# Decoding weights with a parametric relu, loading queries ahead of weights, and another order for the first stage

## The chip, the cores and the metric

The kernel runs on one NeuronCore of one Trainium2 chip. The metric is the device time of one launch in microseconds, lower is better. A time is the median of several runs; beside it stands one execution taken with the hardware profiler, whose rows are read here.

## The reference

```python
# attention over 32 memory slots per head: batch 4, 8 heads, 576 tokens, head_dim 64
a = exp(phi - max over tokens); a = a / (sum over tokens + 1e-09)
k_m = einsum('bhsm,bhsd->bhmd', a, k); v_m = einsum('bhsm,bhsd->bhmd', a, v)
scores = q @ k_m^T / sqrt(64)
attn = softmax(scores) @ v_m                   # tokens: 2304 x 512
x = (attn @ w_a) * (attn @ w_b) @ w_out        # 512 -> 1536 -> 512, gated
h = x @ w_in                                   # 512 -> 2048
out = (h * sigmoid(1.702 * h)) @ w_out2        # 2048 -> 512
```

The attention inputs are float32. The five weight matrices are float64 in memory; the kernel reads them as pairs of 32-bit words.

## The kernel before

**Tiling.** The attention inputs come in eight groups `n = 0..7` (batch `b = n // 2`, four heads each): for each, `phi` (2 DMAs), `k` and `v` (4 DMAs) and `q` (4 DMAs). The weights come in 68 pieces of 128 x 512 elements, called `raw`: 24 of `w_a` and `w_b` together (block `g = 0..5`, four pieces each), 12 of the first output matrix, 16 of `w_in`, 16 of the last one. Each has its own `raw` buffer until it is decoded; there are four such buffers in the first stage.

**Decoding** (`decode_piece`) makes a float32 from the two words of a float64 in four instructions of 128 x 512: ScalarE takes the absolute value of the high word with a scale (L435), VectorE shifts it left by three bits (L437), VectorE puts the sign bit of the high word back (L439), and VectorE adds three bits of the low word (L443).

**Stages.** In the first stage, `memory(n)` and `queries(n)` make the attention of a group, `fold(g, b)` (L791) multiplies the memory values of batch `b` into weight block `g`, and `gated(g, b, u)` (L841, 24 matmuls for each half `u` of the tokens) multiplies the attention by the folded weights; L864 on VectorE multiplies the two results and a DMA stores them (`g1d`). `sum_tokens` (L884, GpSimd) makes sums of them for a Strassen-like product. The second stage (`project`, L1002), the third (`step`, L1277) and the last one (L1478, L1509) are long runs of matmuls. Every matmul is three passes over a high and a low part; `hi_lo` makes these parts with a copy on ScalarE (L341) and a subtraction on VectorE or GpSimd (L335 in `combine`).

**Order.** Nothing is scheduled on the chip. While the program is built, a planner (`Order`) holds a clock for each engine and for the DMAs, gives every instruction an assumed length (`Lengths`, `dve()`, `act()`, `pool()`) and emits instructions in the order in which they would run. Each engine then executes its own list strictly in order, and waits on semaphores where a result isn't there. The SP queue, which issues most DMAs, is such a list too. While nothing else is ready, `warm_up` fills TensorE with small matmuls (L1574) whose result nobody reads, until the first stored result is planned; it holds one of the two PSUM banks of `bank_m`, from which folds and gates also take theirs. `lend_banks` moves banks from the attention's set `bank_a` to `bank_m`. `close_attention` waits for all attention, frees its buffers and marks `close`, after which banks are used in pairs (`pair_up`, `both_free`).

The assumed lengths before are the class's own: 68 ns plus one element a cycle on VectorE. `measured()` sets 150 ns, and further values; it was called at `close` only.

Of the kernel before, what the change touches and what calls it, by code (L numbers as in the profile page):

```python
# [8 lines left out]
F32 = mybir.dt.float32  # L9
# [24 lines left out]
PO1 = 17  # L34
PS1 = 14.8
PT1 = 15
RATE = 330.0, 3000.0
PB1 = 4
PI = 9
# [4 lines left out]
RX = 12  # L44

FIRST = (
    ("phi", 0), ("phi", 1), ("raw", 0), ("kv", 0), ("raw", 1), ("q", 0), ("kv", 1), ("q", 1), ("raw", 2), ("raw", 3),
)


# [22 lines left out]
def dve(n, fast=False):  # L73
    return Lengths.dve + n / (1.92 if fast else 0.96)
# [26 lines left out]
class Order:  # L101
# [9 lines left out]
    def __init__(self):  # L111
        self.clock = {PE: 0.0, ACT: 0.0, DVE: 0.0, POOL: 0.0}
        self.dma, self.marks, self.streams, self.count = 2000.0, {}, [], 0

        self.handicap = {DVE: W0}
        self.rate, self.land = 385.0, 2000.0

    def mark(self, t, *key):
        self.marks[key] = t
# [72 lines left out]
def tile_mem_attention_moe_moe2(  # L192
# [165 lines left out]
    def load(x, n):  # L358
        if x == "raw":
            s = yield "slot", raw_of(n)  # L360
            if s is raw_p and n >= RX:

                od.mark(s[1], "raw_p")
                s = yield "slot", raw_of(n)
            srcs, runs = pieces[n][2:]
            m = 512 // len(srcs)
            for i, src in enumerate(srcs):
                dst = s[0][:, i * m:(i + 1) * m, :]
                (nc.scalar if n < 1 else nc.sync).dma_start(
                    out=dst.rearrange("p (n f) w -> p n (f w)", n=runs), in_=src  # L370
                )
            size = P * 4096
        else:
            s = yield "slot", {"phi": phi_s, "kv": kv_s, "q": q_s}[x]
            if x == "kv":
                for i, src in enumerate((k, v)):
                    load_heads(s[0][:, i], src, n)
            elif x == "phi":
                load_heads(s[0], phi, n, nc.scalar if n == 1 else nc.sync)
            else:  # L380
                b, g = divmod(n, NHG)
                src = q[b].rearrange("(h g) (p c) d -> g h p (c d)", g=NHG, c=QC)[g]
                for h in range(HG):
                    nc.sync.dma_start(
                        out=s[0][h::HG].rearrange("p c d -> p (c d)"), in_=src[h]
                    )
            size = HG * S * {"phi": M, "kv": 2 * D, "q": D}[x] * 4
        loaded[x, n] = s
        od.load(s[1], size, x, n)
# [36 lines left out]
    def decode_piece(t, i, name, part, n, m):  # L426

        raw = loaded.pop(("raw", i))
        lw, hw = (raw[0][:, :, j].rearrange("p (n f) -> p n f", n=n) for j in range(2))
        mf = m[0].rearrange("p (n f) -> p n f", n=n)  # L430
        mu = mf.bitcast(U32)

        slow = Lengths.slow
        t, _ = yield ACT, t, act(512)
        nc.scalar.activation(out=mf, in_=hw.bitcast(F32), func=AF.Abs, scale=2.0 ** -112)  # L435
        t, _ = yield DVE, t, slow * dve(512, True)
        nc.vector.tensor_scalar(out=mu, in0=mu, scalar1=3, scalar2=None, op0=ALU.logical_shift_left)  # L437
        t, _ = yield DVE, t, slow * dve(512)
        nc.vector.scalar_tensor_tensor(  # L439
            out=mu, in0=hw, scalar=0x80000000, in1=mu, op0=ALU.bitwise_and, op1=ALU.bitwise_or  # L440
        )
        t, _ = yield DVE, t, slow * dve(512)
        nc.vector.scalar_tensor_tensor(  # L443
            out=mu, in0=lw, scalar=29, in1=mu, op0=ALU.logical_shift_right, op1=ALU.bitwise_or
        )
        raw_of(i).release(raw, t)
        if name[0] == "wab":
            wt[name] = m
            od.mark(t, *name)
        elif name[0] == "in":  # L450
            decoded[name, part] = m
            od.mark(t, "decoded", name, part)
            if part == 1:
                od.spawn(PW if name[1] else PW0, combine_weights(name[1]))
        elif name[0] == "o2":
            c = name[1]
            t = max(t, (yield "mark", "room", *name))
            t, _ = yield ACT, t, act(DM)
            nc.scalar.activation(out=wo2[c][:, HI], in_=m[0], func=AF.Copy)
            nc.scalar.dma_start(out=w2d[c * P:(c + 1) * P, :], in_=m[0])  # L460
            od.mark(t + 2500.0, "w2d", c)
            t2 = yield from combine(t, wo2[c][:, LO], m[0], f32(wo2[c][:, HI]), ALU.subtract, DM)
            dm_s.release(m, max(t + 2500.0, t2))
            od.mark(t2, "wo2", c)
        else:
            c = name[1]
            decoded[name, 0] = m
            od.mark(t, "decoded", name, 0)
            if c % 4 == 3:
                od.spawn(PS1, combine_out(c // 4))  # L470
# [215 lines left out]

    def lend_banks():

        yield "mark", "attn", 1, 0
        for _ in range(2):  # L690
            s = yield "slot", bank_a
            bank_m.release(s, s[1])

    pair_s = Slots()

    def both_free(i):
        two = [(y, s) for y in (bank_a, bank_m) for s in y.free for x in banks[2 * i:2 * i + 2] if s[0] is x]
        if len(two) < 2:
            return None
        for y, s in two:  # L700
            y.free.remove(s)
        return [s for _, s in two]
# [68 lines left out]
    def fold(g, b):  # L771
# [4 lines left out]
            t = max(t, od.marks["wab", g, r])  # L776
        eff_t[g, b] = s = yield "slot", eff_s
        t = max(t, s[1])
        ps, two = {}, None
        if have("close"):  # L780
            t, two = yield PE, t, 0.0, pair_s
            x = [[two[0][:, c], 0.0] for c in range(NHG)]
        for c in range(NHG):
            if two:
                t, _ = yield PE, t - HOP_PE, (0.0, FOLD / 2)[c]
                ps[c] = x[c]
            else:
                t, ps[c] = yield PE, t - c * HOP_PE, (0.0, FOLD / 2)[c], bank_m
            half = slice(c * D, (c + 1) * D)
            for h in range(HG):  # L790
                nc.tensor.matmul(  # L791
                    ps[c][0][row(h), :], bdv[b][half, h, :], wt["wab", g, h][0][half, :], start=True, stop=True
                )
        for c in range(NHG):
            od.spawn(0, fold_out(t, g, b, c, ps[c], two))
        od.mark(t, "fold", g, b)
# [20 lines left out]
    def gated(g, b, u):  # L817
# [6 lines left out]
            gr_t[g, b] = yield "slot", gr_s  # L824
        gr = gr_t[g, b]
        left, pt, wide = [], [], have("close")
        for j, i in ((0, 0), (1, 0), (0, 1), (1, 1)) if wide else ((0, 0), (0, 1), (1, 0), (1, 1)):
            if True:
                if not wide:
# [19 lines left out]
                if len(pt) == 2:  # L849
                    od.spawn(0, gated_out(g, b, u, slice(0, G1) if wide else slice(j, j + 1), pt, gr, left))  # L850
                    pt = []
        if u == 1:
            eff_s.release(eff_t[g, b], t)

# [752 lines left out]
    with tc.manual_schedule():  # L1607
# [5 lines left out]
            nc.vector.memset(t, 0.0)  # L1613
        make_identity(nc, ident)
        n0 = 2 * NHG
        od.spawn(0, load_all(FIRST))

        nc.scalar.activation(out=zero, in_=zero, func=AF.Exp)
# [48 lines left out]
```

## Time and profile before

| what | value |
|---|---|
| median of 3 runs | 765.1 us (763.99 to 766.24) |
| profiled execution, its own time | 765.62 us |
| its span, first to last instruction | 763.8 us |
| TensorE (PE) busy | 741.0 us, 97% |
| weight loads of TensorE (PEld) | 684.8 us, 90% |
| VectorE (DVE) busy | 615.9 us, 81% |
| ScalarE (ACT) busy | 396.9 us, 52% |
| GpSimd (POOL) busy | 397.3 us, 52% |
| TensorE clock granted | 0.999 of full speed |

Busy TensorE time holds the small filling matmuls too. "PE idle" below is a stretch's length less its PE busy time. The span is 1.8 us shorter than the execution's own time.

### The profile page before, as it was taken

Reading aid. Unit: us, or ns where it says so; the run is one execution under the profiler, and the core shown is the slowest. Engines: PE = TensorE matmul, PEld = TensorE weight load, DVE = VectorE, ACT = ScalarE, POOL = GpSimd, SP = SyncE. Lnnn points to the kernel's source line nnn. Section 1 sums busy time; section 2 is a strip of 40 time slices with the busy share of each in tenths; the row PEclk is TensorE's granted clock in tenths of the full one; section 3 lists DMA queues with packets and bytes.
Section 4 is the critical chain, followed back from the end, with each engine's and each line's share of the span. In section 5 each row is a group of like instructions: output and inputs, shape, how many; then the busy total and the mean of one; then the engine's idle time right before and its main releaser. Section 6 shows DMA issues by size and latency. Waiting matters only on the chain.

```text
span 763.8 us, 14637 instructions
## 1 busy us (share of the span) xinstructions
PE 741.0 (97%) x5360; PEld 684.8 (90%) x5360; DVE 615.9 (81%) x926; ACT 396.9 (52%) x784; POOL 397.3 (52%) x347
## 2 busy tenths in 40 slices
PE   8899999999999989999999999999999999999997
PEld 7676878888788879999989999999998888999997
DVE  4889989699999854974899977767695799998884
ACT  4456654445664354745667555454554456544441
POOL 0213635454987932951899643332151059886661
PEclk9999999999999999999999999999999999999999
DMA  8989583479568796566533845554678956744411
GB/s 256 301 279 313 184 291 136 147 241 317 186 202 256 235 305 192 171 189 189 165 114 101 268 151 181 169 171 147 219 248 278 324 199 190 252 139 139 128 32 36
DMA packets 110360, 153.54 MB, mean 201 GB/s; under 512 B 8400, under 2 KB 89040, under 8 KB 110288
## 3 DMA queue, kind: packets, MB, share of 16 engines
q1 hardware_dynamic: 104832, 143.20, 58.8%
q10 hardware_dynamic: 5456, 9.41, 3.6%
q8 instruction: 42, 0.69, 0.4%
q14 instruction: 30, 0.25, 0.1%
HBM read 100.01 MB, written 52.56 MB: 200 GB/s over the span
## 4 chain that ended last, share of the span: by engine, by line
PE 70%; DVE 9%; DMA 7%; POOL 7%; issue 4%; ACT 2%; SPq 0%; ACTq 0%; DVEq 0%; POOLq 0%
PE bank L1277 23%; PE bank L1509 13%; PE bank L1478 11%; PE bank L1002 11%; PE bank L841 8%; POOL w L335 2%; DMA g1d<-grp 2%; PE bank L791 1%; DMA phi<-in_phi_dram 1%; DVE eff L810 1%; POOL acc L335 1%; DMA acc<-g1d 1%; POOL gr L884 1%; DVE attn L335 1%; DVE acc L439 1%
## 5 line engine op out<-in xcount | busy, mean ns | idle before, releaser
L841 PEld LDWEIGHTS bank<-attn,eff 128*128 128x128 f32 x1152 | 154.5, 188 | 21.2 <-issue 4.4
L841 PE MATMUL bank<-attn,eff 128*128 128x288 f32 x1152 | 165.3, 299 | 2.8 <-DVE acc L864 1.7
L335 POOL TENSOR_TENSOR acc<-acc 128x512 f32<-128x512 f32 (+2 forms) x65 | 95.7, 1494 | 45.0 <-DVE w L335 26.1
L335 DVE TENSOR_TENSOR w<-acc,w 128x512 fp32r<-128x512 f32 (+2 forms) x103 | 106.5, 1060 | 12.4 <-ACT w L341 12.4
L1319 DVE TENSOR_TENSOR acc<-bank,acc 128x384 f32<-128x384 f32 x168 | 88.8, 551 | 32.3 <-PE bank L1277 19.9
L341 ACT ACTIVATE w<-acc 128x512 fp32r<-128x512 f32 (+2 forms) x129 | 74.8, 589 | 51.9 <-PE bank L1509 35.5
L1002 PE MATMUL bank<-attn,w 128*128 128x384 f32 x504 | 93.3, 336 | 3.1 <-DVE attn L335 1.5
L335 DVE TENSOR_TENSOR attn<-acc,attn 128x768 fp32r<-128x768 f32 (+3 forms) x57 | 71.2, 1260 | 28.5 <-ACT attn L341 27.4
L1002 PEld LDWEIGHTS bank<-attn,w 128*128 128x128 f32 x504 | 87.3, 188 | 6.0 <-DVE attn L335 2.8
L341 ACT ACTIVATE attn<-acc 128x768 fp32r<-128x768 f32 (+2 forms) x80 | 61.0, 769 | 53.0 <-PE bank L1002 29.6
L1329 ACT ACTIVATE acc<-acc 128x384 f32<-128x384 f32 x96 | 48.8, 524 | 49.5 <-DVE acc L1319 48.8
L884 POOL TENSOR_TENSOR gr<-gr 128x288 f32<-128x288 f32 x48 | 49.2, 1032 | 31.1 <-DMA g1d<-gr 20.1
L335 POOL TENSOR_TENSOR attn<-acc,attn 128x768 fp32r<-128x768 f32 (+2 forms) x23 | 39.0, 1702 | 47.0 <-ACT attn L341 46.9
L1277 PE MATMUL bank<-attn,w 128*128 128x384 f32 x288 | 55.1, 334 | 0.0
L1277 PEld LDWEIGHTS bank<-attn,w 128*128 128x128 f32 x288 | 50.4, 188 | 0.0
L1002 PE MATMUL bank<-attn,w1b 128*128 128x384 f32 x252 | 48.2, 337 | 1.3 <-DVE attn L335 1.1
L1002 PEld LDWEIGHTS bank<-attn,w1b 128*128 128x128 f32 x252 | 43.8, 188 | 2.8 <-DVE attn L335 2.2
L1277 PE MATMUL bank<-w1b,w 128*128 128x384 f32 x224 | 46.2, 334 | 0.0
L335 POOL TENSOR_TENSOR w<-dm,w 128x256 fp32r<-128x256 f32 x31 | 26.9, 880 | 36.9 <-ACT w L341 36.9
L335 POOL TENSOR_TENSOR w<-acc,w 128x256 fp32r<-128x256 f32 (+2 forms) x24 | 27.4, 1154 | 34.1 <-ACT w L341 34.1
L1277 PE MATMUL bank<-w 128*128 128x384 f32 x224 | 43.8, 334 | 0.0
L1277 PEld LDWEIGHTS bank<-w1b,w 128*128 128x128 f32 x224 | 39.5, 188 | 0.0
(190 smaller groups left out, 1484.7 us busy)
## 6 DMA issues: line engine op xcount, KB each, us to landing
acc<-g1d SPq DMA_DIRECT2D x63, 384.0 KB, 3.8
g2d<-acc SPq DMA_DIRECT2D x96, 192.0 KB, 2.3
raw<-in_moe_w_out_dram SPq DMA_DIRECT2D x24, 512.0 KB, 4.7
acc<-g2d SPq DMA_DIRECT2D x10, 1024.0 KB, 6.7
raw<-in_moe_w_in_dram SPq DMA_DIRECT2D x16, 512.0 KB, 4.4
acc<-g2d SPq DMA_DIRECT2D x16, 512.0 KB, 5.8
g1d<-gr SPq DMA_DIRECT2D x12, 576.0 KB, 3.3
raw<-in_moe_w_a_dram SPq DMA_DIRECT2D x19, 256.0 KB, 4.2
```

Source lines behind the costliest of these rows:

```text
L335: (nc.gpsimd if e == POOL else nc.vector).tensor_tensor(out=dst, in0=in0, in1=in1, op=op)
L341: nc.scalar.activation(out=hi, in_=src, func=AF.Copy)
L439: nc.vector.scalar_tensor_tensor(out=mu, in0=hw, scalar=0x80000000, in1=mu, op0=ALU.bitwise_and, op1=ALU.bitwise_or)
L791: nc.tensor.matmul(ps[c][0][row(h), :], bdv[b][half, h, :], wt["wab", g, h][0][half, :], start=True, stop=True)
L841: nc.tensor.matmul(dst[:, :U], e[:, c, sw, i * CW + j * P:i * CW + (j + 1) * P], attn(b, mv, c, u * U, U), start=(n == 0), stop=(n == 3 * ...
L884: nc.gpsimd.tensor_tensor(out=dst, in0=in0, in1=in1, op=ALU.subtract)
L1002: nc.tensor.matmul(ps[0][:, :N2], w1_of(a, g, sw)[:, r * P:(r + 1) * P], b[0][:, mv, i], start=(first and q == n == 0), stop=(q == NG1 // ...
L1277: nc.tensor.matmul(ps[0][:, :N2], w[:, sw, r, :], y[mv][r], start=(n == 0), stop=(n == 5))
L1319: nc.vector.tensor_tensor(out=s[0], in0=ps[0][:, :N2], in1=x[0], op=ALU.add)
L1329: nc.scalar.activation(out=c[0], in_=c[0], func=AF.Gelu_apprx_sigmoid)
L1478: nc.tensor.matmul(ps[i, s][0], b[0][:, sw, c - o, :], wo2[c][:, mv], start=(c == n == 0), stop=(c == 4 * K4 - 1 and n == 2),)
L1509: nc.tensor.matmul(ps[name][0][:, :NB], x[0][:, sw, c, :], moving(b, h // 2 + c, mv), start=(h == c == n == 0), stop=(h > 0 and c == K4 - ...
```

## The change

The sign step (L439) is gone: the absolute value becomes a parametric relu with a slope of -2^32 for negative inputs, which leaves in the exponent a bit that the shift by three moves into the sign's place. In the table `FIRST` of the first loads, `kv`, `q` of groups 0 and 1 come ahead of all weight pieces; the four DMAs of the first `q` are issued from ScalarE's queue in place of those of the first weight piece. The planner starts with the lengths of `measured()` (with factors of 1.0) and a lower DMA rate. One bank is lent when the first weight block is decoded, the other as before. While a fold or a gate takes single banks, none is taken for a pair.

```diff
+FRONT = 1.0, 1.0, 1.0
+RATE0 = 300.0, 2500.0
...
 FIRST = (
-    ("phi", 0), ("phi", 1), ("raw", 0), ("kv", 0), ("raw", 1), ("q", 0), ("kv", 1), ("q", 1), ("raw", 2), ("raw", 3),
+    ("phi", 0), ("phi", 1), ("kv", 0), ("q", 0), ("kv", 1), ("q", 1), ("raw", 0), ("raw", 1), ("raw", 2), ("raw", 3),
 )
...
-        self.rate, self.land = 385.0, 2000.0
+        self.rate, self.land = RATE0
...
-                (nc.scalar if n < 1 else nc.sync).dma_start(
+                nc.sync.dma_start(
                     out=dst.rearrange("p (n f) w -> p n (f w)", n=runs), in_=src
                 )
...
-                    nc.sync.dma_start(
+                    (nc.scalar if n < 1 else nc.sync).dma_start(
                         out=s[0][h::HG].rearrange("p c d -> p (c d)"), in_=src[h]
                     )
...
-        nc.scalar.activation(out=mf, in_=hw.bitcast(F32), func=AF.Abs, scale=2.0 ** -112)
+        nc.scalar.activation(out=mf, in_=hw.bitcast(F32), func=AF.Prelu, scale=2.0 ** -112, alpha=-2.0 ** 32)
         t, _ = yield DVE, t, slow * dve(512, True)
         nc.vector.tensor_scalar(out=mu, in0=mu, scalar1=3, scalar2=None, op0=ALU.logical_shift_left)
-        t, _ = yield DVE, t, slow * dve(512)
-        nc.vector.scalar_tensor_tensor(
-            out=mu, in0=hw, scalar=0x80000000, in1=mu, op0=ALU.bitwise_and, op1=ALU.bitwise_or
-        )
...
     def lend_banks():
 
-        yield "mark", "attn", 1, 0
-        for _ in range(2):
+        for key in (("wab", 0, 2 * NHG - 1), ("attn", 1, 0)):
+            yield ("mark", *key)
             s = yield "slot", bank_a
             bank_m.release(s, s[1])
 
-    pair_s = Slots()
+    pair_s, single = Slots(), [False]
 
     def both_free(i):
+        if single[0]:
+            return None
...
+        single[0] = not have("close")
         ps, two = {}, None
...
+        single[0] = not wide
...
+        measured()
+        Lengths.pool, Lengths.both, Lengths.slow = FRONT
         od.spawn(0, load_all(FIRST))
```

**The SP queue, from the queries of group 4 on.** `raw_73` here is the eighth weight piece (number 7, the last of block `g = 1`), `phi_95` the next group's `phi`, `g1d<-gr` the stores of the first gate's results. Before:

```order
L384 DMA q_100<-in_q_dram 32x1152 x4
L369 DMA raw_73<-in_moe_w_a_dram 128x512
L369 DMA raw_73<-in_moe_w_b_dram 128x512
L369 DMA raw_74<-in_moe_w_a_dram 128x512
L369 DMA raw_74<-in_moe_w_b_dram 128x512
L869 DMA g1d<-gr 128x2x288
```

Now, with the same loads of group 4 ahead of it:

```order
L386 DMA q_100<-in_q_dram 32x1152 x4
L873 DMA g1d<-gr 128x2x288
L371 DMA raw_73<-in_moe_w_a_dram 128x512
L371 DMA raw_73<-in_moe_w_b_dram 128x512
L873 DMA g1d<-gr 128x288
L352 DMA phi_95<-in_phi_dram 64x4x160
```

The store of gate (0, 0, half 0) has moved ahead of weight piece 7, and that of half 1 ahead of the loads of group 5; pieces 8 and 9 have moved behind group 5.

**TensorE, from the scores of group 1 to the first gate.** L791 is the first fold, in two parts; L841 the first gate; L589 multiplies `k` and `v` of group 2 (`kv_99`, `phi_94`) by its memory weights, and frees the `phi` buffer that group 4 is loaded into; the `ident` matmuls are fillers (L1574) or transposes. Before, in three pieces of that stretch:

```order
L628 MATMUL bank<-qT_108,bdk_93 32x288 x8
L1574 MATMUL bank<-ident 128x128 x8
L548 MATMUL bank<-ident,et_96 128x128 x5
L1574 MATMUL bank<-ident 128x128 x7
L791 MATMUL bank<-acc,gr 32x512 x4
...
L791 MATMUL bank<-acc,gr 32x512 x4
...
L589 MATMUL bank<-kv_99,phi_94 32x128 x20
L548 MATMUL bank<-ident,et_96 128x128 x5
L508 MATMUL bank<-ident,q_101 128x128 x4
L841 MATMUL bank<-attn_81,eff 128x288 x6
```

Now (L626, L546, L792, L844, L587 and L1578 are the same lines, moved):

```order
L626 MATMUL bank<-qT_108,bdk_93 32x288 x8
L1578 MATMUL bank<-ident 128x128 x16
L546 MATMUL bank<-ident,et_96 128x128 x5
L1578 MATMUL bank<-ident 128x128 x2
L792 MATMUL bank<-acc,gr 32x512 x4
L1578 MATMUL bank<-ident 128x128
L792 MATMUL bank<-acc,gr 32x512 x4
...
L1578 MATMUL bank<-ident 128x128 x3
L844 MATMUL bank<-attn_81,eff 128x288 x6
L587 MATMUL bank<-kv_99,phi_94 32x128 x20
```

The two parts of the first fold have moved together, and the first matmuls of the gate stand ahead of the `kv` product of group 2 and not behind it. The whole program has 79 fillers of L1574 instead of 74, and otherwise the same matmuls; each filler is two instructions in the trace.

## Rows read from the trace of the kernel before

**Rows 1.** The page's busy time by engine.
```profile
PE 741.0 (97%) x5360; PEld 684.8 (90%) x5360; DVE 615.9 (81%) x926; ACT 396.9 (52%) x784; POOL 397.3 (52%) x347
```
**Rows 2.** Busy time by stretch, length first, then clock, DMA share, GB/s.
```profile
0.00:64.20 64.20, 55.48 (x689) 45.00 (x689) 46.53 (x116) 33.78 (x84) 12.15 (x19) 1.00 0.88 285
64.20:122.30 58.10, 55.08 (x581) 46.64 (x589) 53.15 (x108) 32.24 (x81) 26.62 (x27) 1.00 0.72 232
122.30:257.60 135.30, 132.81 (x1112) 115.01 (x1112) 121.41 (x166) 69.54 (x124) 91.63 (x82) 1.00 0.66 215
257.60:278.00 20.40, 18.55 (x100) 16.64 (x98) 13.25 (x14) 6.68 (x9) 14.69 (x13) 1.00 0.99 339
278.00:397.00 119.00, 116.51 (x659) 114.04 (x660) 84.45 (x81) 68.80 (x113) 68.95 (x47) 1.00 0.62 180
397.00:764.00 367.00, 362.61 (x2233) 347.42 (x2231) 297.13 (x447) 185.86 (x374) 183.28 (x164) 1.00 0.54 175
```
**Rows 3.** The fillers of L1574 by stretch: PE, then PEld.
```profile
0.00:64.20 64.20, 21.65 (x148) 19.59 (x148) 1.00 0.88 285
```
**Rows 4.** TensorE in order of time: start, length, what.
```profile
37.09 1.06 PE L791 MATMUL bank<-acc,gr 64*32 64x512 f32 x8
...
40.51 1.30 PE L589 MATMUL bank<-kv,phi 128*32 128x128 f32 x40 [0.32 <-ACT phi L326]
...
42.69 1.04 PE L841 MATMUL bank<-attn,eff 128*128 128x288 f32 x6
...
60.76 1.09 PE L791 MATMUL bank<-acc,gr 64*32 64x512 f32 x16
...
64.19 1.04 PE L841 MATMUL bank<-attn,eff 128*128 128x288 f32 x6
```
**Rows 5.** The SP queue in order of time.
```profile
6.57 0.60 SPq L369 DMA_DIRECT2D raw<-in_moe_w_a_dram  x1
...
9.77 2.42 SPq L384 DMA_DIRECT2D q<-in_q_dram  x4
...
41.90 0.64 SPq L350 DMA_DIRECT2D phi<-in_phi_dram  x1
...
49.14 0.52 SPq L369 DMA_DIRECT2D raw<-in_moe_w_a_dram  x1
...
53.14 0.65 SPq L350 DMA_DIRECT2D phi<-in_phi_dram  x1
```
**Rows 6.** The chain that ended last, around weight piece 7.
```profile
49.70 5.13 DMA raw<-in_moe_w_b_dram
54.91 0.69 ACT acc L435
```
**Rows 7.** VectorE in order of time.
```profile
38.46 0.46 DVE L335 TENSOR_TENSOR attn<-aT,attn 128x288 fp32r<-128x288 f32 x1 [0.75 <-ACT attn L341]
...
39.83 1.28 DVE L810 TENSOR_TENSOR eff<-bank,eff 128x512 fp32r<-128x512 f32 x2
...
56.85 0.44 DVE L864 TENSOR_TENSOR gr<-bank,gr 128x288 f32<-128x288 f32 x1
57.21 0.68 DVE L439 SCALAR_TENSOR_TENSOR acc<-raw,acc 128x512 uint32<-128x512 uint32 x1
```
**Rows 8.** The sign step L439 by stretch: VectorE time and count.
```profile
0.00:64.20 64.20, 5.86 (x8) 1.00 0.88 285
...
188.00:278.00 90.00, 12.36 (x11) 1.00 0.74 239
...
sum 764.00, DVE 61.11; mean DVE 10.19
```
**Rows 9.** GpSimd's last sums of the first stage.
```profile
264.80 7.89 POOL L884 TENSOR_TENSOR acc<-acc 128x288 f32<-128x288 f32 x7
```
**Rows 10.** ScalarE in order of time: the first table load.
```profile
0.73 1.28 ACT L1618 ACT_TABLE_LOAD   x1 [0.73 <-PEq L1651]
```
**Rows 11.** The absolute values of L435, largest group by line and shape.
```profile
L435 ACT ACTIVATE acc<-raw 128x512 f32<-128x512 f32 x26 | 17.6, 678 | 22.3 <-DMA raw<-in_moe_w_b_dram 15.2 <-DMA raw<-in_moe_w_out_dram 4.6 <-DMA raw<-in_moe_w_in_dram 2.5
```

More of the change, by code (lines that the diff above doesn't have):

```diff
@@ L793, in fold @@
                 )
+        single[0] = False
         for c in range(NHG):
@@ L851, in gated @@
                     pt = []
+        single[0] = False
         if u == 1:
```

## The prediction

> **What bounds the kernel now.** The page's busy times come first [rows 1]: TensorE at 741.0 of 763.8 us is the bound on average, VectorE comes second. An average over stages says little, so the stretches come next [rows 2]. From 278 to the end TensorE idles 2.5 and 4.2 us in 486, nearly all of the second in the drain of the last outputs. Whatever becomes free on another engine there is worth nothing. So time can only come from ahead of 278, and mostly from the front: in the first 64.2 us TensorE is idle for 8.7 us (64.20 - 55.48), and 21.65 us of its busy time are fillers [rows 3]. Useful work is 55.48 - 21.65 = 33.8 us in 64.2. From 64.2 to 122.3 it idles 3.0 us, to 257.6 another 2.5, to 278 another 1.9.
>
> The start of block (1, 0) at 64.19 divides the two [rows 4]: behind it TensorE has a queue of folds and gates that nearly never runs dry. **The measure of this change is how much earlier that matmul starts,** since all that stands behind it is the same matmuls. What released it is seen in the chain and the DVE rows: weight piece 7 is issued at 49.14 to 49.70 [rows 5], lands 5.13 us later, is decoded on ScalarE from 54.91 [rows 6] and on VectorE, where its sign step at 57.21 stands behind an unrelated product [rows 7]; the fold runs at 60.76, the gate at 64.19 [rows 4]. From landing (54.83) to gate that is 9.4 us. Its issue at 49.14 is bound by the loads of group 4, which began at 41.90 [rows 5], just as the `kv` product of group 2 (40.51 plus 1.30) freed their buffer [rows 4]; ten DMAs take the queue 7.2 us.
>
> **Part by part.**
>
> *First loads.* The same ten items, 6.2 MB, are loaded ahead of group 2, with the last weight piece still last. At the 285 GB/s of the stretch [rows 2] they take about 22 us either way, so piece 3 comes hardly earlier: the four `q` DMAs that leave SP give it 2.42 us [rows 5], the first weight piece takes back about 1. I take 1.4 us. But `q` of group 1 no longer stands behind a weight piece, whose issue held the queue from 6.57 to 9.77, nor behind the first `q`, 2.42 us more [rows 5]. It is issued up to 5.6 us earlier; I take 3 to 5 for the softmax. The four DMAs on ScalarE's queue stand ahead of its first exponential; should one wait for an earlier DMA to land, the exponential and the `kv` product of group 0 wait too. Bounds: nothing, or some 2 us, which the idle 8.7 us ahead of 64.2 would take in.
>
> *The sign step.* 68 instructions, 61.1 us of VectorE [rows 8]; 5.9 us ahead of 64.2, at 0.73 each, of which four, 2.9 us, stand ahead of the first fold. From 278 on they are covered by TensorE's queue and worth nothing. Ahead of that they stand on the path only where a fold waits for a decode, and in 188 to 278, where VectorE is nearly full and eleven of them take 12.4 us [rows 8].
>
> *Parametric relu for absolute value.* The trace has no such instruction. The nearest row is L435, 678 ns for the same shape and engine [rows 11]; bounds are no difference, and double, 46 us of ScalarE, 52% busy [rows 1]. I take no difference. The Trainium skill (ScalarE activation tables: per-element evaluation and per-set limits, What a function is on this engine) speaks of a table load where two functions are in different sets. The row for one load is 1.28 us [rows 10], and by that rule each alternation with the exponential would cost it. The changed program has two table loads, as before, so this term is nothing.
>
> *The order at the front.* Before, the attention's last piece for gate (0, 0) was ready at 38.9 and the folded weights at 41.1 [rows 7]; the gate began at 42.69 [rows 4]. Attention gains the 3 to 5 us of the loads and 2.9 us of sign steps; the weights gain 1.4 us of loading, the same 2.9, and an estimated 2 to 3, as the second part of the fold, which ran at 37.09 [rows 4] behind fillers and transposes, now follows one filler behind the first. Less 6 to 8 us, gate (0, 0) begins at about 35. Now the `kv` product of group 2 stands right behind its first six matmuls, ends at about 37.5, and the loads of group 4 start there instead of at 41.90. Add their 7.2 us: 44.7. The store that now stands ahead of weight piece 7 needs the first half of the gate, 24 matmuls from 35 on, an estimated 7 us among other work, so it is ready. Piece 7 is issued from about 45, lands at 50.8, 4 us earlier. The DMAs hardly allow more: first loads, groups 2 to 4, pieces 4 to 7 and a store are 14.8 MB, 51.9 us at 285 GB/s.
>
> From landing to gate 9.4 us were needed; without the sign step (0.68) and with less in VectorE's way I take 7.2, between 5.5 (the bare sequence of decode, fold, copy and subtraction) and 9.4. Block (1, 0) begins at 58.0, **6.2 us earlier**; bounds 55.5 and 62.
>
> *Banks and pairs.* The earlier bank lets the first gate's matmuls alternate between two banks sooner; that and `single` add no instruction, and I take nothing for them beyond the order.
>
> *64 to 122.* Of 3.0 us idle half goes, with sign steps gone from a VectorE that was busy 53 of 58 us: **1.4 us**, bounds 0 and 3.
>
> *122 to 397.* Idle are 2.5, 1.9 and 2.5 us [rows 2]. GpSimd's last sums end at 272.7 [rows 9], 15 us behind the last gate matmul. If only TensorE came earlier, the second stage would wait for these. But GpSimd works 92 of the 135 us to 257.6 [rows 2], so it has slack to shift with TensorE, and the decodes that it waits for lose eleven sign steps. I take **0.8 us** gained, bounds 4 gained and 4 lost. One rule would enlarge this: the Trainium skill (SBUF — State Buffer, Who interferes with whom) says that a VectorE instruction with two SBUF inputs contends with a GpSimd instruction that reads SBUF. L439 is one; it takes 0.68 us alone [rows 7] and 12.36 / 11 = 1.12 on average in 188 to 278 [rows 8], which agrees. By that rule GpSimd would get back up to 11 x 0.44 = 4.8 us.
>
> **Sum.** 6.2 + 1.4 + 0.8 = 8.4 us from the profiled execution's own 765.6: 757.2. The median of the runs shown lies 0.5 us below that execution; I state 757.
>
> **The rivals.**
>
> *Slower: the first gate is late and holds the queue.* Two stores of gate (0, 0) and the `kv` product of group 2 now stand behind that gate. If it starts as before, at 42.69, the product ends at about 44.8, group 4 loads from there, piece 7 is issued at 52, and the store of half 1, ready at 57.3 [rows 7], stands ahead of group 5, which began at 53.14 [rows 5]. That is 3 us at block (1, 0) and 4 for what follows: 765.6 + 3 to 6, so 769 to 772. It decides from a gate start of about 39.7 on, where the product would end at the old 41.8. For it: in-order queues with stores ahead of loads. Against it: everything that the gate waits for loses VectorE work.
>
> *The gain is given back at the second stage.* TensorE reaches 257 by 6 us earlier, and waits for GpSimd's sums, which stay near 272.7 [rows 9]. Then 1 to 4 us are left: 761.5 to 764.5. For it: GpSimd works 14.7 of the 20.4 us behind the gates. Against it: the same work stood 44 us idle in the 135 before.
>
> *No change: loading bounds the front.* DMA share is 0.88 to 64.2 [rows 2], and piece 7 needs the same bytes as before. If it lands where it did, at about 54, only the decode is faster: 1 to 2 us, 763.5 to 765.
>
> *More than forecast.* Block (1, 0) at 55.5, nothing idle to 122, and three of the 6.9 idle us to 397 gone: 8.7 + 3 + 3, 751 to 753.
>
> **How the numbers follow.** Forecast (754 to 761) 0.60; more than that 0.12; given back 0.12; no change 0.08; slower 0.08. The likeliest is 757. The range of 8 in 10 reaches from 751.5 to 763.5. About 0.3% (2.3 us) is what a measurement of this kernel can tell from no change: faster takes the first two and two thirds of "given back", 0.80; same the rest of it and "no change", 0.12; slower 0.08.
>
> **What would show it.** No L439; L435's successor at about 0.68 us. Gate (0, 0) at about 35, piece 7 landed by 51, block (1, 0) at 56 to 60, the last gate matmul at about 250, and the second stage's stretches as before. Wrong would be: gate (0, 0) after 40, group 4's loads behind 42, or idle time of TensorE ahead of 278 that grows by what the front gained.

## The result, and the profile after

The changed kernel takes 757.95 us (median of 4 runs, 757.21 to 759.21), the kernel before 765.4: a ratio of 0.9906, 95% interval 0.9889 to 0.9923, 7.5 us less. The profiled execution's own time is 757.7 us. The page's busy times, beside [rows 1]:

```profile
PE 741.6 (98%) x5370; PEld 687.0 (91%) x5370; DVE 567.5 (75%) x861; ACT 394.5 (52%) x778; POOL 384.8 (51%) x348
```

Busy time by stretch, cut at the same places of the program as [rows 2], but the second cut stands one fold (16 matmuls, 1 us) later than there (columns: stretch, length, then busy time of TensorE, its weight loads, VectorE, ScalarE, GpSimd, then clock, DMA share, GB/s):

```profile
0.00:62.30 62.30, 56.37 (x693) 46.31 (x693) 42.76 (x110) 32.21 (x81) 16.31 (x24) 1.00 0.89 289
62.30:119.40 57.10, 56.10 (x599) 47.19 (x594) 43.40 (x97) 32.76 (x80) 24.56 (x26) 1.00 0.74 241
119.40:253.50 134.10, 132.80 (x1102) 115.10 (x1098) 106.53 (x145) 69.34 (x123) 91.80 (x87) 1.00 0.72 234
253.50:274.00 20.50, 20.50 (x121) 20.50 (x120) 9.94 (x11) 9.26 (x13) 8.57 (x8) 1.00 0.90 277
274.00:389.00 115.00, 113.10 (x640) 110.38 (x639) 82.52 (x80) 65.72 (x108) 66.19 (x46) 1.00 0.61 177
389.00:756.00 367.00, 362.70 (x2233) 347.51 (x2231) 282.31 (x422) 185.21 (x373) 177.38 (x160) 1.00 0.54 175
```

The last stretch is as long as before, 367 us, so all 7.9 us between the two spans (763.8 and 755.9) were gained ahead of the third stage. TensorE in order of time says where; L844 is the gate, L1006 the second stage, L1281 the third:

```profile
37.40 1.04 PE L844 MATMUL bank<-attn,eff 128*128 128x288 f32 x6
38.37 1.30 PE L587 MATMUL bank<-kv,phi 128*32 128x128 f32 x40
...
58.41 1.07 PE L792 MATMUL bank<-acc,gr 64*32 64x512 f32 x10 [1.49 <-DVE acc L441]
61.11 1.30 PE L587 MATMUL bank<-kv,phi 128*32 128x128 f32 x40 [0.94 <-ACT phi L328]
62.34 1.06 PE L844 MATMUL bank<-attn,eff 128*128 128x288 f32 x6
...
253.49 4.33 PE L1006 MATMUL bank<-attn,w 128*128 128x384 f32 x24
...
388.94 1.20 PE L1281 MATMUL bank<-eff,w 128*128 128x384 f32 x6
```

| point | before | after | gained up to here | predicted |
|---|---|---|---|---|
| gate of block (1, 0) | 64.19 | 62.34 | 1.85 | 6.2 |
| 313th gate matmul | 123.21 | 119.36 | 3.85 | 7.6 |
| first matmul of the second stage | 257.62 | 253.49 | 4.1 | |
| first matmul of the third stage | 396.86 | 388.94 | 7.9 | 8.4 |

Behind each point stands the same work, but for five small transposes at the first. The 313th gate matmul is the one nearest to 122 in [rows 2].

The total came out as forecast, and its parts did not: the front gave 1.85 us and not 6.2, and the second stage, for which almost nothing was forecast, gave 3.8.

### The profile page after: what moved, and what is told of

The parts are those of the page before. It is cut to its first block, busy times and chain, and to the rows that moved or that the text cites. A ratio compares the mean times of both kernels' runs of the same rounds, so it can differ in the third digit from the quotient of the medians.

```text
span 755.9 us, 14604 instructions
## 1 busy us (share of the span) xinstructions
PE 741.6 (98%) x5370; PEld 687.0 (91%) x5370; DVE 567.5 (75%) x861; ACT 394.5 (52%) x778; POOL 384.8 (51%) x348
## 4 chain that ended last, share of the span: by engine, by line
PE 88%; DVE 6%; POOL 2%; issue 1%; ACT 1%; DMA 1%; DVEq 0%; POOLq 0%; ACTq 0%
PE bank L1281 23%; PE bank L844 17%; PE bank L1006 14%; PE bank L1513 13%; PE bank L1482 12%; PE bank L792 3%; PE bank L1578 3%; DVE acc L441 1%; PE bank L587 1%; PE bank L506 1%; DMA raw<-in_moe_w_out_dram 1%; DVE eff L812 1%; DVE attn L337 1%; PE bank L626 1%; POOL attn L337 1%
## 5 line engine op out<-in xcount | busy, mean ns | idle before, releaser
L844 PEld LDWEIGHTS bank<-attn,eff 128*128 128x128 f32 x1152 | 154.5, 188 | 22.5 <-issue 8.1
L844 PE MATMUL bank<-attn,eff 128*128 128x288 f32 x1152 | 166.0, 299 | 2.2 <-DVE eff L812 2.1
L337 POOL TENSOR_TENSOR acc<-acc 128x512 f32<-128x512 f32 (+2 forms) x65 | 94.1, 1469 | 67.1 <-DVE acc L337 27.1
L337 DVE TENSOR_TENSOR w<-acc,w 128x512 fp32r<-128x512 f32 (+2 forms) x104 | 109.3, 1081 | 17.9 <-ACT w L343 17.8
L343 ACT ACTIVATE w<-acc 128x512 fp32r<-128x512 f32 (+2 forms) x129 | 74.6, 590 | 62.6 <-PE bank L1513 34.2
L1006 PE MATMUL bank<-attn,w 128*128 128x384 f32 x504 | 92.1, 335 | 1.5 <-POOL attn L337 0.5
L1006 PEld LDWEIGHTS bank<-attn,w 128*128 128x128 f32 x504 | 87.5, 188 | 3.1 <-POOL attn L337 1.1
L337 DVE TENSOR_TENSOR attn<-acc,attn 128x768 fp32r<-128x768 f32 (+3 forms) x56 | 65.7, 1185 | 29.5 <-ACT attn L343 28.8
L343 ACT ACTIVATE attn<-acc 128x768 fp32r<-128x768 f32 (+2 forms) x80 | 60.7, 768 | 46.2 <-PE bank L1006 38.2
L1281 PE MATMUL bank<-attn,w 128*128 128x384 f32 x288 | 55.1, 334 | 0.0
L888 POOL TENSOR_TENSOR gr<-gr 128x288 f32<-128x288 f32 x48 | 43.5, 907 | 21.8 <-DVE gr L868 8.4
L1281 PEld LDWEIGHTS bank<-attn,w 128*128 128x128 f32 x288 | 50.4, 188 | 0.0
L337 POOL TENSOR_TENSOR w<-acc,w 128x256 fp32r<-128x256 f32 (+2 forms) x23 | 25.6, 1118 | 46.4 <-ACT w L343 46.3
L1006 PE MATMUL bank<-attn,w1b 128*128 128x384 f32 x252 | 48.1, 336 | 0.4 <-DVE attn L337 0.3
L1281 PE MATMUL bank<-w1b,w 128*128 128x384 f32 x224 | 46.2, 334 | 0.0
L1006 PEld LDWEIGHTS bank<-attn,w1b 128*128 128x128 f32 x252 | 43.9, 188 | 1.6 <-DVE attn L337 1.0
L337 POOL TENSOR_TENSOR w<-dm,w 128x256 fp32r<-128x256 f32 x28 | 24.8, 895 | 40.2 <-ACT w L343 40.1
L1281 PE MATMUL bank<-w 128*128 128x384 f32 x224 | 43.8, 334 | 0.0
L337 POOL TENSOR_TENSOR sT<-sT,sm 128x576 f32<-128x576 f32 (+1 forms) x14 | 14.2, 1020 | 51.2 <-DVE sm L652 25.5
```

Of the source, the lines that this page charges most:

```text
L337: (nc.gpsimd if e == POOL else nc.vector).tensor_tensor(out=dst, in0=in0, in1=in1, op=op)
L343: nc.scalar.activation(out=hi, in_=src, func=AF.Copy)
L844: nc.tensor.matmul(dst[:, :U], e[:, c, sw, i * CW + j * P:i * CW + (j + 1) * P], attn(b, mv, c, u * U, U), start=(n == 0), stop=(n == 3 * ...
L888: nc.gpsimd.tensor_tensor(out=dst, in0=in0, in1=in1, op=ALU.subtract)
L1006: nc.tensor.matmul(ps[0][:, :N2], w1_of(a, g, sw)[:, r * P:(r + 1) * P], b[0][:, mv, i], start=(first and q == n == 0), stop=(q == NG1 // ...
L1281: nc.tensor.matmul(ps[0][:, :N2], w[:, sw, r, :], y[mv][r], start=(n == 0), stop=(n == 5))
```

## The experiments

Three theories were set against each other. **Theory 1:** VectorE's work is what was gained. **Theory 2:** the new loads, lengths and order at the front are. **Theory 3**, formed after the first eight runs: a gain at the front is kept or given back at the start of the second stage, by where ScalarE's list puts two copies there, ahead of the time at which their space comes free or behind it.

All twelve runs together; the points are from the profiled execution of each, which for the second and third run held 3.4 us at a granted clock of 0.50 from 29.2 and 30.5 us on, so their points ahead of the second stage are left out. "Second block" is the 49th gate matmul: block (1, 0), in the two runs with the old lending (0, 1). "Second stage takes" is the time from its first matmul to the third stage's, 139.2 in the kernel before.

| run | median, us | ratio to before (95%) | first gate | second block | second stage begins | second stage takes |
|---|---|---|---|---|---|---|
| changed kernel | 757.95 | 0.9906 (0.9889 to 0.9923) | 37.40 | 62.34 | 253.49 | 135.5 |
| decode alone, old order | 756.89 | 0.9899 (0.9864 to 0.9934) | 40.23 | 61.32 | 251.64 | 135.6 |
| the same, 24 first-stage pieces | 762.94 | 0.9958 (0.9937 to 0.9979) | | | | 139.3 |
| the same, 44 later pieces | 761.25 | 0.9941 (0.9909 to 0.9973) | | | | 135.9 |
| decode alone, replanned | 761.98 | 0.9950 (0.9925 to 0.9974) | 39.27 | 60.66 | 256.44 | 137.9 |
| all but the decode | 762.64 | 0.9968 (0.9948 to 0.9988) | 39.46 | 66.72 | 254.79 | 138.8 |
| old lengths | 762.59 | 0.9972 (0.9955 to 0.9988) | 35.05 | 52.95 | 249.68 | 142.7 |
| old first loads | 759.94 | 0.9933 (0.9912 to 0.9955) | 38.67 | 61.90 | 249.57 | 142.9 |
| old banks | 768.91 | 1.0046 (1.0028 to 1.0065) | 40.52 | 65.86 | 261.52 | 136.2 |
| old lending only | 764.57 | 0.9988 (0.9972 to 1.0004) | 40.16 | 65.82 | 259.92 | 136.2 |
| old first loads, copies later | 754.26 | 0.9865 (0.9835 to 0.9895) | 38.52 | 61.76 | 249.94 | 135.5 |
| old lengths, copies later | 756.16 | 0.9877 (0.9850 to 0.9903) | 34.50 | 52.34 | 250.89 | 136.5 |
| block 1 decoded first | 762.36 | 0.9956 (0.9932 to 0.9980) | 37.26 | 64.70 | 251.85 | 142.7 |

**The decode alone in the old order.** The kernel before, with its planner's old steps, so that every other instruction keeps its place:

```diff
-        nc.scalar.activation(out=mf, in_=hw.bitcast(F32), func=AF.Abs, scale=2.0 ** -112)
+        nc.scalar.activation(out=mf, in_=hw.bitcast(F32), func=AF.Prelu, scale=2.0 ** -112, alpha=-2.0 ** 32)
...
         t, _ = yield DVE, t, slow * dve(512)
-        nc.vector.scalar_tensor_tensor(
-            out=mu, in0=hw, scalar=0x80000000, in1=mu, op0=ALU.bitwise_and, op1=ALU.bitwise_or
-        )
```

> The kernel before, every instruction in its old place, but without the 68 sign steps and with the parametric relu in place of the absolute value. Theory 1, VectorE's work is what was gained (in the first stage and ahead of the second): most of the 7.4 us of the change, 5 to 7 us, so 758 to 760. Theory 2, the new order at the front is what was gained: loads and matmuls are where they were, and 1 to 3 us come, 762 to 764. Under both, block (1, 0) starts 1 to 2 us earlier than 64.19, since only the decode of its last piece is shorter.

It took 756.89 us, as much as the whole change gives, which is what theory 1 forecast for this run and more than theory 2 did. So the decode alone is enough; that the rest gives nothing does not follow, and it is measured below. What changed on the engines is seen in GpSimd's sums of the kernel before (duration: minimum, median, maximum in ns), then in this run's busy times and its sums:

```profile
L884 POOL TENSOR_TENSOR gr<-gr x48: 797/986/1589, 62.3 to 260.3; 128x288 f32<-128x288 f32 x48
L884 POOL TENSOR_TENSOR acc<-acc x32: 797/1130/1519, 158.7 to 271.3; 128x288 f32<-128x288 f32 x32
```

```profile
PE 739.2 (98%) x5360; PEld 685.6 (91%) x5360; DVE 565.7 (75%) x858; ACT 398.0 (53%) x784; POOL 387.6 (51%) x347
```

```profile
L889 POOL TENSOR_TENSOR gr<-gr x48: 794/824/1568, 59.4 to 253.3; 128x288 f32<-128x288 f32 x48
L889 POOL TENSOR_TENSOR acc<-acc x32: 799/896/1622, 155.6 to 264.8; 128x288 f32<-128x288 f32 x32
```

The same 347 GpSimd instructions in the same order take 9.7 us less (397.3 in [rows 1], 387.6 here), and the median sum falls from 986 to 824 and from 1130 to 896 ns. The means fall less, from 1032 to 972 and from 1063 to 1022 ns, and the shortest stay: of these 80 sums, 31 take over 1000 ns and not 39. The only thing that is gone is a VectorE instruction that reads two tiles of SBUF. That agrees with the Trainium skill (SBUF — State Buffer, Who interferes with whom), which has such an instruction contend with GpSimd's reads.

**First-stage pieces, or later ones.** The same edit for pieces below 24, then for the others:

```diff
+        new = i < 24
...
+        new = i >= 24
```

> The same for the 24 pieces of w_a and w_b alone; the other 44 keep the absolute value and the sign step. If the gain of the sign step is at the front and with the first blocks, this holds all of it, as much as with all 68 pieces. If it is at the start of the second stage, where twelve pieces of the first output matrix are decoded, it holds less than half, 0 to 2 us.

> The other half: the 44 later pieces lose the sign step, the 24 of w_a and w_b keep it. If the second stage's start is where the gain comes from, 2 to 4 us, with GpSimd's last sums ending earlier than 272.7. If it comes from the front, nothing, within 0.5 us of before. Pieces behind 278 are worth nothing under either.

Ratios of 0.9958 and 0.9941 lie 0.42% and 0.59% below one, and 1.01% for all 68 pieces: the two parts add up, within intervals of 0.2 to 0.35% to either side. So some 3.2 us come from the pieces that the front and the gates wait for, and 4.5 from the later ones. The first part is a little under half, so both places matter. The second stage tells them apart: it takes 139.2 us before, 139.3 with the first-stage pieces changed, 135.9 with the later ones and 135.6 with all. What it waits for is seen on ScalarE, whose copies make its operands out of GpSimd's sums, which were stored and are loaded again (`acc<-g1d`). From 248 to 300 these copies wait for such loads (us in all, times, longest), before, with first-stage, later and all pieces:

```profile
ACT attn L341 <- DMA acc<-g1d: 14.4, 6, 3.5
ACT attn L341 <- DMA acc<-g1d: 14.7, 6, 3.5
ACT attn L341 <- DMA acc<-g1d: 8.2, 4, 3.0
ACT attn L341 <- DMA acc<-g1d: 6.2, 3, 2.9
```

GpSimd's last sums end at 272.7, 272.8, 270.1 and 265.6, which is 15.1, 15.2, 13.7 and 14.0 us behind the stage's first matmul. TensorE itself waits most for VectorE's part of the same operands (L335): 2.6, 2.9, 1.3 and 1.1 us from 245 to 400. So the second stage's gain, 3.3 to 3.6 us, is that of the later pieces: with them its operands are ready earlier. In the changed kernel ScalarE's wait for the loads is 1.6 us.

**The decode alone, replanned, and all but the decode.** In the first the planner's step goes too; the second is the changed kernel with the old four instructions:

```diff
-        t, _ = yield DVE, t, slow * dve(512)
-        nc.vector.scalar_tensor_tensor(
-            out=mu, in0=hw, scalar=0x80000000, in1=mu, op0=ALU.bitwise_and, op1=ALU.bitwise_or
-        )
```

> The kernel before with the new decode as the planner orders it (so that it knows of the sign step's absence), but the old first loads, lengths, banks. Theory 1 (VectorE's work): as with the old order, 5 to 7 us gained, 758 to 760. Theory 2 (front order): 1 to 3 us, 762 to 764. Rival: planning without the sign step gives an order that by chance is worse than the old one, 765 or more; then the new lengths and loads are needed to have the gain.

> All of the change but the decode: absolute value and sign step are back, and the planner knows of them. Theory 1 (VectorE's work is the gain): 763 to 765, at most 2 us faster than before. Theory 2 (loads, lengths and order at the front): 759 to 761. Both add up to the whole if they are independent.

Neither theory had these numbers. Replanned, about half of the decode's gain is lost (0.9950 against 0.9899; the intervals just overlap), though nothing but the planner's choices differs. The rest of the change alone gives 0.32%. The decode in the old order and the rest, 0.9899 and 0.9968, would make 0.987 if they were independent. The changed kernel holds the decode as the planner places it, and 0.9950 with 0.9968 makes 0.992, which lies in the interval of the whole, 0.9906 (0.9889 to 0.9923). So in the changed kernel both theories have a share, by these ratios about three fifths for the decode and two fifths for the rest.

**Single settings undone in the changed kernel.** Lengths and rate, first loads and queues, then both halves of the bank edit:

```diff
-RATE0 = 300.0, 2500.0
+RATE0 = 385.0, 2000.0
...
-        measured()
-        Lengths.pool, Lengths.both, Lengths.slow = FRONT
```

> The changed kernel with the planner's old lengths and DMA rate; loads, banks and decode as changed. If the measured lengths put the first gate ahead of the kv product of group 2 and so freed the loads of group 4 earlier, that is gone: gate (0, 0) near 40, block (1, 0) 1 to 2 us later, 759 to 760. If they do nothing, 758. Rival: the old lengths are better for the middle, and the time is under 757.

```diff
-    ("phi", 0), ("phi", 1), ("kv", 0), ("q", 0), ("kv", 1), ("q", 1), ("raw", 0), ("raw", 1), ("raw", 2), ("raw", 3),
+    ("phi", 0), ("phi", 1), ("raw", 0), ("kv", 0), ("raw", 1), ("q", 0), ("kv", 1), ("q", 1), ("raw", 2), ("raw", 3),
```

> The changed kernel with the old order of the first loads and the old choice of queues for them. By the prediction's step (3 to 5 us earlier q of group 1, 1.4 us for the weights) the first gate starts 2 to 4 us later than 37.4; at the end that is worth 1 to 2 us: 759 to 760. Rival: the first gate is held by weights, not by attention, and the time stays 758.

```diff
-        for key in (("wab", 0, 2 * NHG - 1), ("attn", 1, 0)):
-            yield ("mark", *key)
+        yield "mark", "attn", 1, 0
+        for _ in range(2):
...
-        if single[0]:
-            return None
```

> The changed kernel without the earlier lending of a bank and without the rule that keeps single banks from pairs. The prediction took nothing for them: 757.5 to 758.5. Rival: the earlier bank lets the first gate's matmuls alternate between banks, and without it the gate and so the store ahead of piece 7 are later: 759 to 761.

With the old lengths the front is far better, not worse: gate (0, 0) at 35.05, the next block at 52.95, the second stage entered 3.8 us earlier than in the changed kernel; and the median is 4.6 us higher. What eats it is at the second stage. ScalarE, then TensorE, then windows around it, in this run:

```profile
258.05 0.85 ACT L343 ACTIVATE attn<-acc 128x768 fp32r<-128x768 f32 x1 [1.18 <-PE bank L1006]
258.80 0.47 ACT L1028 ACTIVATE gr<-bank 128x384 f32<-128x384 f32 x1
266.68 0.49 ACT L1028 ACTIVATE gr<-bank 128x384 f32<-128x384 f32 x1 [7.41 <-DMA g1d<-gr]
267.07 2.30 ACT L343 ACTIVATE attn<-acc 128x768 fp32r<-128x768 f32 x3
```

```profile
262.19 2.24 PE L1006 MATMUL bank<-attn,w 128*128 128x384 f32 x12
267.96 1.01 PE L1006 MATMUL bank<-attn,w 128*128 128x384 f32 x2 [3.53 <-ACT attn L343]
269.85 3.57 PE L1006 MATMUL bank<-attn,w 128*128 128x384 f32 x10 [0.89 <-POOL attn L337]
```

```profile
249.70:264.40 14.70, 14.70 (x86) 14.41 (x84) 6.26 (x6) 3.77 (x5) 10.84 (x11) 1.00 0.91 307
...
266.50:273.30 6.80, 4.45 (x13) 3.95 (x14) 3.38 (x3) 2.80 (x5) 1.82 (x1) 0.50 0.34 104
```

L1028 copies the first product out of its bank, into the space of `gr`. The second of two such copies waits 7.41 us, until the last sums have been stored from that space. L343, which makes the operands of the next products, stands behind it in ScalarE's list, and TensorE waits 3.53 us for it. From 266.5 on the granted clock is 0.50, the 1.2 GHz level, for 6.8 us: ten matmuls take 3.57 us there, twelve had taken 2.24. With the old first loads the same copy waits 6.87 us, TensorE 2.99, and the clock is 0.50 for 6.8 us as well.

The old banks make the kernel slower than before, and the prediction had taken nothing for them. The first gate is at 40.52, and the planner takes block (0, 1) second, which needs the attention of groups 2 and 3; block (1, 0) comes third, and weight piece 7 is issued at 53.35, behind group 5's `k` and `v`, and not at 47.90. To part the two halves of that edit, one run keeps the rule on pairs and undoes the lending alone:

> The changed kernel without the earlier lending of a bank, but with the rule that keeps single banks from pairs. Without both the time was 768.9, 11 us over the changed kernel's. If the lending is what matters (an order at the front with later folds), 765 to 769 here; if the rule is what matters (pairs that starve the single banks at the close of attention, near 142), 757 to 760.

At 764.57 us the lending is worth 6.6 us and the rule on pairs the other 4.3. Without the lending TensorE waits for an exponential from 56.5 on, and the clock falls there too, to 0.50 for 10.2 us; first the row, then the window:

```profile
60.24 1.11 PE L567 MATMUL bank<-ident,et 128*128 128x128 f32 x4 [3.71 <-ACT et L559]
```

```profile
58.00:68.20 10.20, 6.98 (x61) 6.05 (x61) 8.04 (x17) 2.87 (x8) 4.66 (x5) 0.50 0.49 166
```

**The copies later.** The planner is told that the space of `gr` comes free 8 us later than it thought, so that four more operand copies stand ahead of the two L1028; on the kernels with the old first loads and with the old lengths:

```diff
-        give(hc_s, views(p2_m, N2, 7))
+        hc_s.free += [[x, now() + 8000.0] for x in views(p2_m, N2, 7)]
```

> The changed kernel with the old first loads, in which TensorE came to the second stage at 249.6 and then waited 4.3 us, because two copies of the first product stood in ScalarE's list ahead of the operands of the third and waited 6.9 us for a buffer whose last sums were still being stored. Here the planner is told that this buffer comes free 8 us later, so that eight operand copies stand ahead of these two and not four. Theory 3 (the front's gain is given back at that wait, by an order that another placing mends): the second stage takes 136 to 138 us and not 142.9, the third starts at 386 to 388, and the time is 754 to 757, less than the changed kernel's 758. Rival: GpSimd's sums, which end at 262, are themselves what the stage waits for; the wait moves to another operand and the time stays at 759 to 761.

> The same edit on the changed kernel with the old lengths, where block (1, 0) started at 53 and TensorE came to the second stage at 249.7, and waited 4.4 us there, after which its granted clock was 0.5 for 6.8 us. Theory 3: that wait and the clock's fall go, 5 to 6 us, so 756 to 758. Rival (sums bound): 761 to 763.

Both come out as theory 3 has it: 759.94 becomes 754.26, 762.59 becomes 756.16. GpSimd's sums still end at 261.7 and 262.9, so the end of the sums by itself did not hold the stage. ScalarE and the second stage's first 24 us, for the old first loads:

```profile
266.62 0.85 ACT L343 ACTIVATE attn<-acc 128x768 fp32r<-128x768 f32 x1 [1.23 <-PE bank L1006]
267.38 1.23 ACT L1028 ACTIVATE gr<-bank 128x384 f32<-128x384 f32 x3
```

```profile
249.90:274.00 24.10, 24.10 (x141) 24.10 (x140) 10.63 (x12) 10.85 (x15) 12.79 (x10) 1.00 0.85 271
```

No copy waits, TensorE has no idle time, the clock stays at 1.00.

In the changed kernel the two copies stand where they do in the kernels that wait, behind four operand copies of this stage, and do not wait: GpSimd has finished the sums of `gr` by 246.9 and makes those of `acc` last. With the old lengths it makes those of `gr` last, until 261.0, and with the old first loads and block 1 first until 262.0 and 264.2. The changed kernel's ScalarE and GpSimd, then GpSimd with the old lengths:

```profile
262.59 0.85 ACT L1028 ACTIVATE gr<-bank 128x384 f32<-128x384 f32 x2
243.43 3.46 POOL L888 TENSOR_TENSOR gr<-gr 128x288 f32<-128x288 f32 x4 [0.99 <-DMA g1d<-gr]
```

```profile
251.72 9.30 POOL L888 TENSOR_TENSOR gr<-gr 128x288 f32<-128x288 f32 x8
```

So two things together make the wait: copies early in ScalarE's list, and sums of `gr` late in GpSimd's. Placing the copies later mends it; placing the sums earlier was not run by itself.

At 754.26 us the kernel with the old first loads and the copies later has the lowest median of all; its interval touches those of the changed kernel and of the decode alone, against which it was not run directly.

**Block 1 decoded first.** A higher priority for block `g = 1`:

```diff
-PG = (10.3, 13.5, 14.5, 16.5, 16.6, 16.7)
+PG = (10.3, 10.35, 14.5, 16.5, 16.6, 16.7)
```

> The changed kernel with a higher priority for the weights of block g = 1 (13.5 becomes 10.35), so that the decode of piece 7 stands on VectorE ahead of transposes and sums of group 3; the program is the same up to the first gate. By the prediction's own measure (landing to gate 7.2 us, all behind block (1, 0) the same) it starts 3 to 4 us earlier than 62.34 and the end follows by as much: 754 to 755. By what the kernel with the old lengths showed, where this block began 9 us earlier and the later points did not follow, the work that made way is owed later: the block starts earlier, but 360 gates are done at 126 to 128 as before, and the time is 756 to 760.

It did not do what it was made for: the decode that releases the second block's fold began on ScalarE at 58.48, behind copies of another fold, where it had begun at 55.90, and the profiled execution had 3.4 us at a granted clock of 0.50 from 53.5 on. So it says nothing on that step. It is one more case of theory 3: the second stage begins 1.6 us earlier than in the changed kernel, a copy L1028 waits 6.88 us, TensorE 3.01, the clock is 0.50 for 6.8 us, and the stage takes 142.7 us.

## Why the prediction was right, point by point

- **The sum, 8.4 us, and 757:** right in size (7.9 between the spans, 757.95 measured), with its terms wrongly divided. That the forecast time held is in good part luck: the first term was 4.35 us too large, the second 0.6 and the third 3.3 too small.
- **"Block (1, 0) earlier", 6.2 us:** mis-sized, 1.85. Gate (0, 0) began at 37.40 and not 35, the `kv` product of group 2 ended at 39.7 and not 37.5, so group 4 was loaded from 39.77 and piece 7 issued at 47.90 and not 45. The mechanism was as told: the product stands right behind the first gate's matmuls and the loads start with its end. The SP queue of the changed kernel:

```profile
39.77 0.64 SPq L352 DMA_DIRECT2D phi<-in_phi_dram  x1
...
47.00 0.53 SPq L873 DMA_DIRECT2D g1d<-gr  x1
47.90 0.34 SPq L371 DMA_DIRECT2D raw<-in_moe_w_a_dram  x1
48.30 0.42 SPq L371 DMA_DIRECT2D raw<-in_moe_w_b_dram  x1
```

- **"From landing to gate I take 7.2":** it stayed at the upper bound, 9.4. The piece landed 4.6 us behind its issue at 48.30, at 52.9, the gate ran at 62.34. The sign step's 0.68 us was saved, but the decode now waited in two lists: on ScalarE until 55.90, behind a fold's copies and two of the queries, and on VectorE until 56.67, behind a transpose. Between the fold and the gate stood the `kv` product of the next group, which waited 0.94 us for ScalarE:

```profile
53.97 1.08 ACT L810 ACTIVATE eff<-bank 128x512 fp32r<-128x512 f32 x2 [1.66 <-PE bank L792]
54.94 1.10 ACT L328 ACTIVATE qT<-bank 128x512 f32<-128x512 f32 x2
55.90 0.70 ACT L437 ACTIVATE acc<-raw 128x512 f32<-128x512 f32 x1
```

```profile
55.98 0.77 DVE L673 STREAM_TRANSPOSE aT<-sT 128x576 f32<-128x576 f32 x1
56.67 0.48 DVE L439 TENSOR_SCALAR acc<-acc 128x512 uint32<-128x512 uint32 x1
```

- **What brought the first gate forward (5.3 us):** from runs with one part undone, the sign step 2.1 (39.46 without it), the early lending of a bank 2.8 (40.16), the first loads 1.3 (38.67), while the lengths cost 2.4 (35.05). They don't add up to 5.3, since each run has an order of its own. The prediction had 2.9 for the sign step, 3 to 5 and 1.4 for the loads, 2 to 3 for the order, and nothing for the bank, which was the largest.
- **"All that stands behind it is the same matmuls":** wrong as a measure. In the change itself that matmul moved 1.85 us and the end 7.9. With the old lengths and the copies later, block (1, 0) starts at 52.34, 10 us earlier than in the changed kernel, and the second stage only 2.6 us earlier. The planner had drawn that block ahead of other work (449 matmuls without fillers stand ahead of it there, 533 in the changed kernel), and this was still owed: the 361st gate matmul runs at 127.1 there and at 126.9 in the changed kernel.
- **Idle time from 64 to 122, 1.4:** 2.0 us were gained there (3.85 less 1.85).
- **From 122 to 397, 0.8:** mis-sized, 4.1, at the upper bound of 4. To the second stage 0.3, within it 3.8: TensorE's idle time to the third stage fell from 4.3 us [rows 2] to 1.9, and the other 1.4 us are busy time of the same matmuls (135.1 to 133.6), which no run explains. GpSimd's last sums ended at 262.8, 10 us earlier than in [rows 9]:

```profile
258.10 4.66 POOL L888 TENSOR_TENSOR acc<-acc 128x288 f32<-128x288 f32 x4 [1.10 <-DMA g1d<-acc]
```

  The rule on shared access to SBUF had been named as what would enlarge this term, at up to 4.8 us; the run with the old order shows 9.7 us of GpSimd's time over the whole program.
- **The parametric relu at no price, and the table loads:** right, a median of 670 ns beside 678 on average [rows 11], still two table loads:

```profile
L437 ACT ACTIVATE acc<-raw x26: 656/670/702, 22.8 to 599.6; 128x512 f32<-128x512 f32 x26
```

- **The rivals:** "given back at the second stage" did not happen in the changed kernel, but in four of its relatives (old lengths, old first loads, block 1 first, and in part the replanned decode). Its cause there was not that the operands waited for GpSimd's sums, as the prediction had it, but that two copies ahead of them in ScalarE's list waited for the space of the sums of `gr`. "The first gate is late", which was to decide from 39.7 on, was not seen either: with the old banks the gate came at 40.52, but the planner then put the `kv` product ahead of it and group 4 was loaded from 39.67, as in the changed kernel. The loss there, to 768.91 us, came by another way, most likely the order of the blocks, with waits of 3.71 and 3.84 us and a lower clock around their ends; no run parts these.

What stays open: whether the sums come earlier because GpSimd's instructions are shorter or because VectorE's results, which they need, are ready earlier; and what makes the changed kernel better than the replanned decode. It is not the places of a few copies alone: of the 5.4 us between the two at the third stage's first matmul, 3.0 are there when the second stage begins (253.49 against 256.44).

## What to carry to other kernels

Take an instruction out with the order held fixed before judging a change that also lets a planner reorder: here the instruction alone was worth 1.0%, and the same removal, replanned, half of it. A gain at the front is worth what arrives at the next stage that every path passes through; look there for a copy that waits for a buffer and has operands queued behind it, since moving that copy paid 5.7 and 6.4 us between the medians. Measure at points with equal work behind them, not at the start of one block.

## What was not expected of the hardware

A wait of TensorE of 3 to 3.7 us cost more than its length in five runs: around its end began a stretch at a granted clock of 0.50 (6.8 us with waits of 2.99, 3.53 and 3.01 us near 264 to 270, 6.8 and 10.2 us with 3.71 us from about 56.5). The length of the wait does not tell whether it comes: the kernel before waited 3.15 us at 26.8 and its clock stayed at 1.00, while at the same place waits of 2.58 and 2.88 us (first-stage pieces, later pieces) had 3.4 us at 0.50 around or behind their ends, and so had one of 3.84 us with the old banks. In two runs such a stretch began at 58.8 (all but the decode, 6.8 us) and 53.5 (block 1 first, 3.4 us) though TensorE's waits just ahead of it were no longer than 0.90 and 1.43 us. The granted clock explains only a part of each loss: half of the 6.8 us at most. With the old first loads the one execution with a mean granted clock of 0.999 took 756.62 us, and the five at 0.995 to 0.997 took 758.7 to 761.3; by that one execution, an estimate, some 3 of the 5.7 us that the later copies gave back are the clock's.

Taking out a VectorE instruction with two operands in SBUF shortened the median GpSimd sum by 162 and 234 ns, a sixth to a fifth, but the mean by 60 and 41 ns only, and GpSimd's whole busy time by 9.7 of 397.3 us.
